# An RWKV-5 recurrence with a routed MoE behind it: in-place state decay, a gate on one partition, a split first block, the first-layer weights in one tile, a split last store and a new instruction order

## The chip, the cores and the metric

The kernel runs on one core of one Trainium2 chip. The metric is the device time of one execution in microseconds (us); less is better. A run more than 1.5% above the fastest of the same kernel is called slow, and only fast runs are compared with fast runs. A ratio quoted here is the mean time of the fast runs of one kernel over the mean time of the fast runs of the kernel before in the same rounds on the same chip, so it is not quite the ratio of the medians beside it.

Engine names in profile lines: PE is the matrix engine, PEld its weight loads, DVE the vector engine, ACT the scalar engine, POOL the GpSimd engine, SP the engine that queues most transfers (SPq is its queue).

## The reference, cut to what matters

```python
# r, k, v: [4, 8, 768, 48]; w, u: [8, 48]
for t in range(S):
    cur = einsum('bhd,bhe->bhde', u[None] * k_t, v_t)
    y[:, :, t] = einsum('bhd,bhde->bhe', r_t, state + cur)
    state = w[None, :, :, None] * state + einsum('bhd,bhe->bhde', k_t, v_t)
x = y as [4, 768, 384]
# one expert of eight for each batch element, chosen by the mean of x
logits = x.mean(axis=1) @ w_gate
e = argmax(logits); gate_w = softmax(logits)[e]
out = gate_w * (relu(x @ w1[e]) @ w2[e])      # w1: [8, 384, 1024], w2: [8, 1024, 384]
```

The inner einsum over `d` is a recurrence over 768 steps. The expert of a batch element is known only when its whole sequence is done.

## The kernel before

The sequence is cut into 12 blocks of 256 steps, three for each of the four batch elements. For each block the kernel scales `k` and `r` by powers of the decay, transposes them on PE (`t`, tile `twp`), copies them out (`kr`), computes scores on PE (`at`), multiplies them by a mask on DVE (`gt`, 1.2 us, the largest DVE operation), and adds up `y` and the state `s` on PE. When a batch element is done, the gate picks its expert, POOL issues the load of that expert's weights, and the two matmul layers of the expert (`mm1`, tile `hp`; `mm2`, tile `op`) run among the blocks of the following elements.

Every instruction is a step with a name, and a string, the order table, says in which order the steps are emitted on all engines:

```python
ORDER = """\
DVE k 0 0; DVE r 0 0; ACT late; fill 1 b0; PE t 0 0 b0; DVE k 0 1; DVE r 0 1; J k 0; J r 0
POOL r 1; fill 2 b1; PE t 0 1 b1; ACT kr 0 1; ACT v 0; DVE kr 0 0; fill 6 b2; PE at 0 0; DVE k 1
...                                   # some 90 more lines
```

Inside one engine the order is fixed; engines wait for each other by semaphores, which a framework places from the tiles and the address ranges that instructions touch. `fill` puts matmuls of zeros on PE to keep its clock up.

The parts that the change touches:

```python
def carried(g):                      # state of the last block back into PSUM
    nc.tensor.matmul(out=s_ps[b][:, 0 : 2 * D * NP], lhsT=ident,
                     rhs=carry[b]..., start=True, stop=False)

def state_out(g, o):                 # o = 1: the decayed state, as bf16
    st = work.tile([128, NP, 2 * D], BF16, tag="st")
    nc.vector.tensor_mul(st, s_ps[b]..., wcmask if o else bmask...)

def gate(b):                         # logits on all 128 partitions
    for ct in range(NCT):
        nc.tensor.matmul(out=lgp, lhsT=pools[b][:, ct : ct + 1].to_broadcast([128, 128]),
                         rhs=wg[:, ct, :], ...)

def weights(b):
    for fh in range(2):              # w1 in two tiles, each with its own transfer
        t = wpool.tile([128, NCT, HF], BF16, tag=f"w1_{fh}")
        nc.gpsimd.dma_start(out=t, in_=moe_w1[...][:, :, HF * fh : HF * fh + HF])
        w1s[b, fh] = t
    ...                              # w2 in one transfer

step(("fence",), {"SP": 0.5}, lambda e: nc.sync.dma_start(out=fence, in_=gws[0][0:1, :]), ...)
```

The fence is a tiny transfer that reads the gate weight of batch element 0. It stands in SP's queue ahead of the loads of blocks 7 to 9, so that these do not compete with the first expert's weights.

Of the kernel before, what the change touches and what calls it, by code (L numbers as in the profile page):

```python
# [19 lines left out]
DVE k 0 0; DVE r 0 0; ACT late; fill 1 b0; PE t 0 0 b0; DVE k 0 1; DVE r 0 1; J k 0; J r 0  # L20
POOL r 1; fill 2 b1; PE t 0 1 b1; ACT kr 0 1; ACT v 0; DVE kr 0 0; fill 6 b2; PE at 0 0; DVE k 1
DVE prod 0 0 b0; DVE prod 0 1 b1; DVE gt 0 0; PE t 1 0 b2; ACT kr 1 0; PE s 0 0; DVE st 0 1
PE bonus 0; PE t 1 1 b0; PE at 0 1; PE y 0 1 0; PE s 0 1; PE inter 0 1; ACT kr 1 1
DVE prod 1 0 b2; DVE gt 0 1; DVE prod 1 1 b0; POOL k 2; POOL r 2; DVE tcol 0; J vt 0; SP load 4
SP load 5; SP load 6; fill 2 b1; PE at 1 0; PE bonus 1; DVE tcol 1; DVE st 1 0; ACT v 1
POOL vt 1; DVE gt 1 0; PE t 2 1 b1; PE y 0 1 1; PE t 2 0 b2; PE carry 1; PE s 1 0; PE y 0 0 0
PE vt_y 0; PE at 1 1; DVE st 1 1; POOL k 3; POOL r 3; ACT kr 2 1; ACT kr 2 0; ACT xn 0 1
DVE gt 1 1; DVE prod 2 0 b2; DVE prod 2 1 b1; PE y 0 0 1; PE y 1 1 0; PE s 1 1; ACT xn 0 0
PE y 1 0 0; PE inter 1 0; PE at 2 0; DVE gt 2 0; PE y 1 0 1; PE inter 1 1; PE bonus 2
PE t 3 1 b0; PE at 2 1; PE turn 0 b2; DVE tcol 2; DVE st 2 0; POOL v 2; POOL vt 2; POOL k 4  # L30
POOL r 4; DVE gt 2 1; PE t 3 0 b1; PE vt_y 1; PE pool 0; PE carry 2; PE y 1 1 1; PE s 2 0
ACT v 3; ACT kr 3 1; ACT xn 1 0; ACT xn 1 1; DVE kr 3 0; DVE prod 3 1 b0; DVE st 2 1
DVE prod 3 0 b1; PE y 2 0 1; PE y 2 1 0; PE at 3 0; PE turn 1 b0; PE bonus 3; PE inter 2 1
PE y 2 0 0; PE y 2 1 1; PE vt_y 2; DVE gt 3 0; PE at 3 1; ACT v 4; ACT xt 0 b2; ACT xn 2 1
DVE tcol 3; DVE xt 1 b0; DVE gt 3 1; PE inter 2 0; ACT xn 2 0; PE t 4 1 b1; PE pool 1; PE pool 2
DVE gate_sums 0; PE t 4 0 b2; PE gate 0; ACT kr 4 1; ACT kr 4 0; DVE k 5; DVE choose 0
POOL vt 3; POOL r 5; POOL weights 0; ACT exp 0; fill 3 b0; PE at 4 0; DVE prod 4 0 b2
DVE prod 4 1 b1; DVE gt 4 0; POOL v 5; PE turn 2 b0; PE t 5 0 b2; ACT xt 2 b0; ACT kr 5 0
PE s 3 0; PE t 5 1 b1; ACT kr 5 1; DVE st 3 1; PE at 4 1; PE bonus 4; PE s 3 1; PE vt_y 3
PE inter 3 1; DVE gt 4 1; DVE st 4 0; DVE tcol 4; PE at 5 0; ACT xn 3 0; ACT xn 3 1  # L40
DVE prod 5 0 b2; DVE prod 5 1 b1; PE inter 4 0; PE carry 4; PE s 4 0; PE bonus 5
PE mm1 0 2 0 b0; PE mm1 0 3 0 b2; ACT relu 0 2 0 b0; PE mm1 0 2 1 b1; ACT relu 0 3 0 b2
ACT relu 0 2 1 b1; POOL k 6; POOL vt 4; DVE gt 5 0; DVE r 6; DVE tcol 5; PE mm1 0 0 0 b0
PE t 6 1 b2; PE t 6 0 b1; DVE st 4 1; DVE gw 0; DVE kr 6 1; DVE prod 6 1 b2; PE s 4 1; PE vt_y 4
PE at 5 1; DVE st 5 0; ACT relu 0 0 0 b0; ACT kr 6 0; DVE prod 6 0 b1; PE turn 3 b0
PE mm1 0 3 1 b2; ACT xt 3 b0; DVE xn 4 0; PE carry 5; PE mm1 0 6 0 b1; PE inter 4 1
PE mm1 0 4 0 b0; ACT relu 0 3 1 b2; DVE relu 0 6 0 b1; ACT relu 0 4 0 b0; PE inter 5 0
PE mm1 0 1 1 b2; ACT relu 0 1 1 b2; DVE gt 5 1; DVE xn 4 1; PE mm1 0 0 1 b1; PE mm1 0 5 1 b0
PE mm1 0 1 0 b2; ACT relu 0 0 1 b1; ACT relu 0 5 1 b0; PE s 5 0; DVE st 5 1; PE at 6 0
PE mm1 0 6 1 b1; DVE relu 0 1 0 b2; DVE gt 6 0; SP fence; SP load 7; SP load 8; SP load 9  # L50
PE mm1 0 7 1 b0; PE mm1 0 5 0 b2; DVE relu 0 7 1 b0; DVE r 7; ACT relu 0 6 1 b1
ACT relu 0 5 0 b2; POOL vt 5; POOL k 7; POOL r 8; PE mm1 0 4 1 b1; PE inter 5 1; PE s 5 1
PE at 6 1; PE vt_y 5; ACT v 6; ACT relu 0 4 1 b1; POOL k 9; DVE xn 5 1; PE mm1 0 7 0 b2
PE t 7 0 b0; PE pool 4; PE bonus 6; PE pool 3; PE mm2 0 5 0 b1; ACT relu 0 7 0 b2; DVE xn 5 0
DVE gt 6 1; PE pool 5; DVE gate_sums 1; PE mm2 0 5 1; DVE k 8; ACT v 7; ACT kr 7 0; PE gate 1
DVE choose 1; DVE prod 7 0 b0; PE mm2 0 1 0 b2; PE mm2 0 1 1; DVE tcol 6; ACT gated 0 5 b1
DVE vt 6; ACT gated 0 1 b2; PE t 7 1 b1; PE mm2 0 4 0 b0; PE mm2 0 4 1; PE t 8 0 b2; DVE kr 7 1
DVE prod 7 1 b1; ACT exp 1; ACT gated 0 4 b0; ACT kr 8 0; DVE r 9; PE s 6 0; PE at 7 0
PE turn 5 b1; ACT xt 5 b1; PE mm2 0 0 0 b0; PE mm2 0 0 1; DVE gt 7 0; DVE prod 8 0 b2
POOL weights 1; DVE gated 0 0 b0; PE bonus 7; PE t 9 1 b1; PE t 9 0 b2; PE t 8 1 b0; ACT v 8  # L60
ACT kr 8 1; DVE st 6 1; PE s 6 1; PE at 7 1; PE vt_y 6; ACT kr 9 0; ACT xn 6 0; DVE kr 9 1
DVE prod 9 1 b1; DVE tcol 7; DVE prod 8 1 b0; DVE st 7 0; DVE prod 9 0 b2; DVE gt 7 1; POOL vt 7
PE mm2 0 3 0 b1; PE mm2 0 2 0 b0; PE mm2 0 2 1; PE carry 7; PE inter 7 0; PE inter 6 1
# [52 lines left out]
def kernel(  # L116
# [250 lines left out]
    def transpose_by_dma(g, i):  # L367

        if g not in krs:
            kr_tile(g)  # L370
# [555 lines left out]
```

## Time and profile before

Three runs took 137.63 to 137.73 us. The first profile fell on an execution with a wait, which the prediction below takes out by calculation. A later profile of the same kernel (run e0 below, 137.75 us) serves as "before" from here on.

| part of the 137.75 us | us | how it is read |
|---|---|---|
| front: start of the span to the first expert matmul | 37.22 | start of the first `hp` row in PE's timeline |
| dense part: first expert matmul to the end of the last | 93.60 | 124.96 + 5.86 - 37.22 in the lines below |
| tail: last eviction and last store | 5.3 | the span, 136.1, less 130.82 |
| outside the span | 1.65 | 137.75 - 136.1 |

In PE's timeline the columns are start, duration, engine, line, operation, tiles, engine shape, sizes, count, and in brackets the idle time before it with what ended it.

```profile
37.22 2.14 PE L669 MATMUL hp<-xt,w 128*128 128x384 bf16 x12 [0.68 <-DMA w<-in_moe_w_dram]
```

The end of its chain of waits (start, duration, what):

```profile
124.96 5.86 PE op L688 x36
130.90 0.58 ACT ob L699
```

Twelve expert matmuls start together after a short wait of 0.68 us and run at full clock. The chain ends with one eviction by ACT, and the store follows.

### The profile page before, as it was taken

To read this page: it belongs to the slowest core of one execution; us is meant where nothing else is said; L and a number is where in the kernel's file an instruction comes from. 1 tells how busy PE (TensorE), PEld (TensorE's weight loads), DVE (VectorE), ACT (ScalarE), POOL (GpSimd) and SP (SyncE) were. 2 spreads that over 40 slices of the span, in tenths; PEclk is the share of its full clock that TensorE was granted. 3 is DMA by queue.
4 is the path that set the end of the run, shared out by engine and by line. 5 is a ranking of instruction groups with operands and counts; after the bars stand their busy time and mean duration, and the time that the engine had idled before them with its cause. 6 is when DMAs were issued, how large, how long until landed. Compare 5 with 4: busy or idle time off the path is not lost.

```text
span 139.8 us, 4473 instructions
## 1 busy us (share of the span) xinstructions
PE 129.2 (92%) x1928; PEld 89.4 (64%) x1928; DVE 98.5 (70%) x193; ACT 67.6 (48%) x119; POOL 55.2 (39%) x52
## 2 busy tenths in 40 slices
PE   6998999998589999999999999999999999999940
PEld 2256677876347676778767786686767756666620
DVE  6499999996946689988659978857756336683110
ACT  0986584677235747376446483073544600422130
POOL 4158599969940537142101963804120060000000
PEclk9999999999968999999999999999999999999997
DMA  2999997979999999089649992995006559980254
GB/s 47 293 325 325 285 237 198 244 205 247 206 209 240 237 293 280 1 105 212 137 95 270 319 271 72 128 212 115 5 0 170 172 80 191 235 284 5 66 130 144
DMA packets 46473, 25.47 MB, mean 182 GB/s; under 512 B 39284, under 2 KB 45429, under 8 KB 46453
## 3 DMA queue, kind: packets, MB, share of 16 engines
q1 hardware_dynamic: 41332, 18.89, 49.9%
q0 software_dynamic: 4288, 6.29, 26.3%
q8 instruction: 15, 0.25, 0.7%
q10 hardware_dynamic: 832, 0.00, 0.3%
q14 instruction: 6, 0.04, 0.2%
HBM read 26.76 MB, written 4.72 MB: 225 GB/s over the span
## 4 chain that ended last, share of the span: by engine, by line
PE 65%; SPq 15%; DMA 10%; DVE 3%; issue 2%; POOL 1%; ACT 0%; POOLq 0%; ACTq 0%
PE op L688 23%; PE hp L669 22%; SPq L176 14%; DMA w<-in_moe_w_dram 5%; DMA r<-in_r_dram 5%; PE twp L351 4%; PE y L498 3%; PE xp L582 2%; PE at L402 2%; PE s L526 2%; PE y L468 2%; PE y L486 1%; DVE rp L333 1%; PE s L616 1%; SPq L206 1%
## 5 line engine op out<-in xcount | busy, mean ns | idle before, releaser
L669 PE MATMUL hp<-xt,w 128*128 128x384 bf16 x192 | 37.8, 338 | 2.0 <-DMA w<-in_moe_w_dram 2.0
L680 ACT ACTIVATE ht<-hp 128x384 bf16<-128x384 f32 x45 | 21.5, 490 | 34.0 <-PE hp L669 34.0
L688 PE MATMUL op<-w,ht 128*128 128x384 bf16 x192 | 34.0, 326 | 0.0
L415 DVE TENSOR_TENSOR gt<-at,mask 128x1024 bf16<-128x1024 f32 x24 | 29.2, 1217 | 1.3 <-PE at L402 1.0
L669 PEld LDWEIGHTS <-w 128*128 128x128 bf16 x192 | 20.2, 115 | 10.9 <-DMA w<-in_moe_w_dram 2.0
L688 PEld LDWEIGHTS <-ht 128*128 128x128 bf16 x192 | 18.1, 98 | 11.0 <-DVE tcol L441 0.2
L333 POOL TENSOR_TENSOR kp<-k,dk 128x768 bf16<-128x768 f32 x8 | 14.7, 1841 | 15.6 <-DMA k<-in_k_dram 15.6
L446 POOL TENSOR_TENSOR vt<-vb,tcol 128x768 bf16<-128x768 bf16 x9 | 14.0, 1551 | 16.3 <-DVE tcol L441 11.5
L339 ACT COPY kr<-twp 128x1024 bf16<-128x1024 bf16 x16 | 16.0, 1014 | 6.9 <-PE twp L351 6.9
L333 POOL TENSOR_TENSOR rp<-r,dr 128x768 bf16<-128x768 f32 x7 | 12.7, 1818 | 5.9 <-DMA r<-in_r_dram 5.8
L701 DVE TENSOR_SCALAR ob<-op,gw 128x384 f32<-128x384 f32 x13 | 7.9, 615 | 9.5 <-PE op L688 9.4
L498 PE MATMUL y<-vb,gt 64*128 64x48 bf16 x384 | 14.4, 180 | 0.2
L498 PEld LDWEIGHTS <-gt 64*128 64x128 bf16 x384 | 11.4, 93 | 3.9 <-issue 2.6
L682 DVE TENSOR_SCALAR ht<-hp 128x384 bf16<-128x384 f32 x19 | 10.2, 554 | 5.4 <-PE hp L669 5.3
L699 ACT ACTIVATE ob<-op,gw 128x384 f32<-128x384 f32 x11 | 6.4, 581 | 14.3 <-PE op L688 14.3
L654 POOL DMA_DIRECT2D w<-in_moe_w_dram x8 | 6.4, 803 | 15.7 <-DVE xt L341 9.4
L351 PE MATMUL twp<-ident,rp 128*128 128x128 bf16 x96 | 9.5, 223 | 0.8 <-POOL rp L333 0.7
L390 DVE TENSOR_TENSOR prod<-twp,kr 128x512 bf16<-128x512 bf16 x24 | 9.7, 418 | 0.7 <-ACT kr L339 0.5
L351 PE MATMUL twp<-ident,kp 128*128 128x128 bf16 x96 | 9.6, 225 | 0.6 <-DVE kp L333 0.4
L526 PE MATMUL s<-vb,kp 64*128 64x96 bf16 x160 | 10.2, 204 | 0.0
L402 PE MATMUL at<-kr 48*64 48x128 bf16 x384 | 9.9, 220 | 0.3 <-DVE gt L415 0.2
L339 ACT CAST xn<-y 128x384 bf16<-128x384 f32 x15 | 6.9, 482 | 5.1 <-PE y L486 3.5
(75 smaller groups left out, 168.6 us busy)
## 6 DMA issues: line engine op xcount, KB each, us to landing
k<-in_k_dram SPq DMA_DIRECT2D x12, 384.0 KB, 5.1
r<-in_r_dram SPq DMA_DIRECT2D x12, 384.0 KB, 6.3
v<-in_v_dram SPq DMA_DIRECT2D x12, 384.0 KB, 5.6
out_dram<-ob SPq DMA_DIRECT2D x22, 192.0 KB, 3.4
w<-in_moe_w_dram POOLq DMA_DIRECT2D x8, 384.0 KB, 6.3
w<-in_moe_w_dram POOLq DMA_DIRECT2D x4, 768.0 KB, 10.1
out_dram<-ob SPq DMA_DIRECT2D x4, 96.0 KB, 2.1
wuT<-in_w_dram ACTq DMA_DIRECT2D x2, 0.8 KB, 2.8
```

The costliest lines, as they stand in the source:

```text
L176: nc.sync.dma_start(out=t.rearrange("q h c d -> q h (c d)"), in_=src[b, :, L * gi : L * gi + L, :].rearrange("h (q c) d -> q h (c d)", c=2),)
L333: eng.tensor_mul(dst[:, cs, :, 0:D].rearrange("q c h d -> q h c d"), src[:, :, cs, :], dec[:, :, cs, :])
L339: nc.scalar.copy(dst, src)
L351: nc.tensor.transpose(out=twp[:, o + p, :], in_=src[:, c, 2 * p : 2 * p + 2, :].rearrange("s a b -> s (a b)"), identity=ident,)
L402: nc.tensor.matmul(out=at[64 * j : 64 * j + 64, a, pp, cs, :].rearrange("q (c i) -> q c i", c=2), lhsT=kt[q, p, j, cs, :], rhs=rt[q, p, j] ...
L415: nc.vector.tensor_mul(gts[g][:, rnd].rearrange("q a p c t -> q (a p) (c t)"), ats.pop((g, rnd)).rearrange("q a p c t -> q (a p) (c t)"), ...
L446: eng.tensor_mul(vts[g], vbs[g].rearrange("q c h d -> q (c h) d"), src.to_broadcast([128, 2 * H, D]))
L498: nc.tensor.matmul(out=yj[:, D * h : D * h + D], lhsT=gt[q, p // 2, a, p % 2, c, :], rhs=vb[q, c, h, :], start=begin(g, j), stop=(c == 1), ...
L526: nc.tensor.matmul(out=sp[:, 96 * p : 96 * p + 96], lhsT=kp[g % NR][qo, c, 2 * p : 2 * p + 2, :].rearrange("s a b -> s (a b)"), rhs=vb[qo, ...
L669: nc.tensor.matmul(out=hp[:, 0:SB].rearrange("q (n l) -> q n l", l=C), lhsT=w1s[b, ft // 4][:, ct, ft % 4 :: 4], rhs=xts[b][:, 3 * sb : 3 ...
L680: nc.scalar.activation(out=o, in_=src, func=ACT.Relu)
L688: nc.tensor.matmul(out=moe_ps[b, si][:, 0:DM], lhsT=hts[b][:, ft, 128 * si : 128 * si + 128], rhs=w2s[b][:, ft, :], start=(ft == 0), stop= ...
```

## The change

The intent: save PE's identity matmuls that carry the state, and most of the gate's fp32 matmuls; start block 0 earlier; shorten the last store; and anneal the order table anew for the new durations. The table differs in nearly every line, so it is not shown. The core of the rest:

```diff
-def carried(g): ...                                  # identity matmul, 8 of them
+def decay(g):                                        # the state decays where it lies
+    sp = s_ps[g // NB][:, 0 : 2 * D * NP]
+    nc.vector.tensor_mul(sp, sp, wcmask...)
 def state_out(g, o, eng):
-    nc.vector.tensor_mul(st, s_ps[b]..., wcmask if o else bmask)
+    if o: copy(eng, st, sp)                          # bf16 copy, ACT or DVE
+    else: nc.vector.tensor_mul(st, sp, bmask...)

-    lgp = s_ps[b][:, ...];   lhsT=pools[b][:, ct : ct + 1].to_broadcast([128, 128])
+    lgp = s_ps[b][0:1, ...]; lhsT=pools[b][:, ct : ct + 1]
+def gate_spread(b, bank):                            # gate weight to 128 partitions
+    nc.tensor.matmul(out=gwp[b][:, 0:1], lhsT=one, rhs=gw1[b], start=True, stop=True)
+def gate_spread_out(b): nc.vector.tensor_copy(gws[b], gwp.pop(b)[:, 0:1])

-    for fh in range(2):
-        t = wpool.tile([128, NCT, HF], BF16, tag=f"w1_{fh}")
-        nc.gpsimd.dma_start(out=t, in_=moe_w1[...][:, :, HF * fh : HF * fh + HF])
-        w1s[b, fh] = t
+    t = wpool.tile([128, NCT, F], BF16, tag="w1")
+    for f in ([slice(0, HF), slice(HF, F)] if b == 0 else [slice(0, F)]):
+        nc.gpsimd.dma_start(out=t[:, :, f], in_=src[:, :, f])
+    for fh in range(2):
+        w1s[b, fh] = t[:, :, HF * fh : HF * fh + HF]

-    fence reads gws[0][0:1, :]
+    fence reads gw1[0]
... # block 0: scalings, transposes, copies and products by halves of the heads
... # last output: ACT and DVE evict 192 columns each, each half stored from another queue
... # x kept as [128, 3, 768] instead of by chunks; an output store is one transfer, not two
```

## The prediction

> **What bounds the kernel now.** I read the page first, then the timelines of TensorE (PE), VectorE (DVE) and GpSimd (POOL), then the chain of waits. From the page, busy shares and four rows of the forty slices (3.5 us each):
>
> ```profile
> PE 129.2 (92%) x1928; PEld 89.4 (64%) x1928; DVE 98.5 (70%) x193; ACT 67.6 (48%) x119; POOL 55.2 (39%) x52
> ...
> PE   6998999998589999999999999999999999999940
> ...
> DVE  6499999996946689988659978857756336683110
> ...
> PEclk9999999999968999999999999999999999999997
> DMA  2999997979999999089649992995006559980254
> ```
>
> The reader is to see two stages. From slice 3 to 10 DVE stands at 9 and so, nearly, does the DMA; there PE is busy partly with filler matmuls. From slice 13 on PE is at 9 throughout and DVE falls off. Between lies one hole, with a low clock after it. The timelines of POOL and PE show the hole:
>
> ```profile
> 30.15 1.82 POOL L333 TENSOR_TENSOR rp<-r,dr 128x768 bf16<-128x768 f32 x1 [1.06 <-DMA r<-in_r_dram]
> 31.95 1.71 POOL L654 DMA_DIRECT2D w<-in_moe_w_dram  x2
> ```
> ```profile
> 36.56 0.36 PE L432 MATMUL s<-U,prod 128*128 128x8 bf16 x8
> 38.87 3.71 PE L669 MATMUL hp<-xt,w 128*128 128x384 bf16 x12 [1.95 <-DMA w<-in_moe_w_dram]
> ```
>
> POOL scales the r of block 5 when its load lands, and only then issues the first expert's weights; they land 6.9 us later. PE waits 1.95 us for them, and its first twelve matmuls take 3.71 us where twelve at the later rate of 0.163 us (1.95 us for x12 in the chain) take 1.95: 1.76 us lost to a half clock. After that the chain is PE matmuls almost without a break, to the last output:
>
> ```profile
> 45.53 0.16 PE s L508
> ...
> 47.00 1.95 PE hp L669 x12
> ...
> 83.85 0.62 PE s L616 x6
> ...
> 134.59 0.58 ACT ob L699
> ```
>
> The profiled execution took 141.46 us (its span 139.8, so 1.66 lie outside the span) and the timed ones 137.65. Taking out both losses gives 139.8 - 1.95 - 1.76 + 1.66 = 137.75. So I read the timed runs as having neither the hole nor the slow clock: the DMA is faster without the profiler, and the weights are there when PE gets to them at 36.9. The three timed runs agree within 0.1 us, which also speaks against a wait on DMA. The timed run then is: 36.9 us of front, 95.65 - 1.76 = 93.9 us of dense PE (38.87 to 134.52, less the slow clock), 5.3 us of tail, 1.66 us outside.
>
> **What the Trainium skill says.** "TensorE: Matmul & The Clock Gate", section "LDWEIGHTS (loading the stationary operand)": the load costs by the columns of the stationary operand, not by its rows. The gate loads 128 fp32 columns at 190 ns each in this trace against 98 to 115 ns for 128 bf16 columns; with one column it should nearly vanish. The same page, "Why this matters for your kernels", asks for no PE gaps over about 3 us to keep the clock; here 1.95 us sufficed (granted clock 0.56 from 38.8 to 42.4), so the measurement decides. "PSUM — Partial Sum Buffer", "The four PSUM rules": writes of VectorE leave the accumulate bits alone, so the matmul after an in-place decay adds onto the decayed state; the kernel before never does this, so its trace shows nothing of it. "Trainium Kernel Development and Optimization", "Key Constraints": queues of several engines share the same 16 DMA engines, and issuing from several only saves issue time. In the trace a store of 96 KB costs some 0.6 us to issue, and the last output issues two in a row.
>
> **The change part by part.**
>
> Decay in place. It removes 8 identity matmuls that carry the state back into PSUM, 0.16 us each in the chain: 1.3 us of PE, 5 of them (0.8) after the first expert matmul. On DVE it is neutral: 8 multiplications of 0.55 us become 8 decays of the same shape. It adds 8 copies to bf16, 0.48 us each as ACT's casts of that size; the new order puts 6 on ACT (2.9 us for an engine that is 48% busy) and 2, of blocks 5 and 8, on DVE (0.55 each). The state's path gets one hop longer, which matters only in the front.
>
> Gate on one partition. Its six matmuls cost about 0.61 us in the chain; 0.13 us is what six one-column bf16 matmuls cost there (the pooling sums), so I put 0.25 for fp32. Saved: 0.36 x 4, three of them (1.1) late. The broadcast of the weight adds one fp32 matmul, by estimate 0.2 us (0.6 late), and one DVE copy of 0.17 us per batch. DVE's small operations keep their 0.13 to 0.17 us: they are fixed cost.
>
> Block 0 by halves of the heads. Before, the scores need both transposes copied out, and DVE puts the scaling of k1 (2.57 us beside POOL; 1.0 us when alone) and two products ahead of the first mask multiplication, which starts at 12.21 us. After, k1 is on POOL and half the heads suffice. But each half now needs both position columns of the decay table, so the first scaling waits for the third table activation, at 7.03 instead of 6.01. Step by step: four scalings of 0.52 us pitch to 9.2, one half copy of 0.45 to 9.65, product to 10.1, first mask at about 10.2: 2.0 us earlier.
>
> Order of the front. DVE binds there: 12.1 busy of the 12.6 us from 7.4 to 20. From its first mask multiplication to that of block 4's second half (start 33.87, end 35.1) it takes 22.9 us. I added up its list in the new order: 10 mask multiplications at 1.22, 9 products at 0.41 or so, 7 state operations at 0.55, the vt of blocks 0 and 2 at 0.95, v1 at 0.55, small ones 1.6: 23.4 us, of which 22 pass at the pitch of before (operations overlap by some 6%). xt 1, k5 and one kr copy have left DVE. So that mask ends at about 32.5 with half a microsecond of stalls, and PE is ready for the first expert matmul near 33.7 instead of 36.9. It also has less behind it: one group of y and s matmuls, one bonus and one inter group now come after that point, 0.50 + 0.18 + 0.17 = 0.85 us moved.
>
> The weights then bind. POOL must do k5 as well as r5 before it issues them, and the fence that held back loads 7 to 9 opens earlier, because the gate weight it waits for moves ahead in DVE's order (before, SP waited 8.8 us for it, until 40.1). So nothing speeds the landing except the earlier choice of the expert (about 28 instead of 30.3 by the same sums) and POOL's shorter list ahead. In timed runs they land by 36.9 at the latest before; I put 34.9 after, between 33.5 and 37.
>
> Dense part: 93.9 - 0.8 (carries) - 1.1 (gates) + 0.6 (spreads) + 0.85 (moved) = 93.45.
>
> Tail: the last output is evicted by two engines at once, 192 columns each: about 0.35 instead of 0.58 us, and the second issue of 0.6 us goes to another queue: 5.3 - 0.23 - 0.6 = 4.4 us.
>
> Sum: 34.9 + 93.45 + 0.3 (stalls for the second half of the weights, needed only some 2.6 us after the first) + 4.4 + 1.66 = 134.7 us, 2.1% less than before.
>
> **The rivals.** First, a hole in front of the experts: PE is ready 3 us sooner but the weights come as late as before (36.9). For it: POOL's k5, the early fence, DMA at 9 in that stretch, and the hole in the profiled run. Against it: the narrow timed runs. The front's gain is then void, and the total is 136.7; with a half clock after the hole another 1.7, so 138.4 at worst. Second, the front is not DMA-bound at all without the profiler and the weights land by 33.7: then 133.5, and near 132.5 if the new order also removes stalls later on. For it: the rate falls from 325 GB/s early on to about 200 to 240 later at the same busy share, as if something else, perhaps the profiler, took the engines' time. Third, DVE or ACT becomes the bound later, through 2.9 us more on ACT and the longer state path; against it, DVE is busy at most 13 of 15 us in any stretch after 45 us, ACT 8.7, and matmuls of the experts fill every wait. I give that at most 1 us.
>
> **Range and chances.** The certain part is the tail (0.9) and the leaner dense part (0.45 after the moved work): 1.4 us, 1%. The rest depends on the landing of the weights. The mark for 2% is 134.9, right at my number. I put 132.9 to 136.7 as the range of 8 in 10; faster by over 2%: 0.52; within 2%: 0.45; slower: 0.03.
>
> **What would show it.** In the profile after: the first mask multiplication near 10.2; no identity matmul between state updates; a gate of 0.25 us; the first expert matmul ready near 33.7 to 36 and a wait of 2 to 3 us for weights still there, as the profiler's runs have slow DMA, with a low clock behind it; 93 to 94 us from the first to the last expert matmul at full clock; a tail of 4.4 us. I am wrong if the first mask comes later than 11.5, if the weights land after 37 in timed runs, or if PE waits on DVE or ACT by more than 1 us in the dense part.

## The result, and the profile after

The changed kernel took 146.34 us (median of four; fast runs 145.40, 146.28, 146.40) against 137.64 for the kernel before in the same rounds. The ratio is 1.0615 with a 95% interval of 1.056 to 1.0671: slower by 6%. The prediction of 134.7 was wrong, and so was its range.

The page of the changed kernel, a fast run of 146.28 us (its span 144.6; one digit is the busy share in tenths of a slice of 3.6 us):

```profile
PE 130.1 (90%) x1927; PEld 89.3 (62%) x1929; DVE 93.2 (64%) x189; ACT 74.2 (51%) x136; POOL 58.4 (40%) x52
...
PE   6989989799319999999899999999999999999970
...
DVE  6275999989800587789966998894667614165120
...
PEclk9999999999955999999999999999999999999997
DMA  3999999995999894007999397089810069980043
```

PE has a hole in the eleventh and twelfth slice ("31"), and its clock is halved in the twelfth and thirteenth ("55"). DVE starves just behind it ("00"), for nothing comes from PE, while the transfers ("99894") are busy all along: something is being loaded, and PE waits for it. PE's timeline there:

```profile
37.89 0.35 PE L680 MATMUL hp<-xt,w 128*128 128x384 bf16 x1 [0.55 <-DMA w<-in_moe_w_dram]
42.79 2.75 PE L680 MATMUL hp<-xt,w 128*128 128x384 bf16 x8 [4.55 <-DMA w<-in_moe_w_dram]
```

Where the kernel before ran twelve expert matmuls in a row, here one runs, then PE waits 4.55 us for weights, and the next eight take 0.34 us each instead of 0.18. Counted from the second matmul the run divides so: front 42.79, dense part 97.3 (to 140.06), tail 4.5, outside the span 1.7; sum 146.3. Against the table of before that is +5.6, +3.7, -0.7 and 0.

The transfers in that stretch come from two queues. POOL's timeline of the changed kernel has the issue of the first expert's `w1`:

```profile
32.54 1.71 POOL L667 DMA_DIRECT2D w<-in_moe_w_dram  x2 [0.76 <-issue]
```

SP's queue in the changed kernel (start, duration of the issue, what):

```profile
32.91 0.69 SPq L923 DMA_DIRECT2D fence<-gw  x1
...
34.71 3.88 SPq L180 DMA_DIRECT2D v<-in_v_dram  x1
38.68 6.03 SPq L180 DMA_DIRECT2D k<-in_k_dram  x1
```

SP's queue in the kernel before, in its first profile:

```profile
40.10 0.70 SPq L888 DMA_DIRECT2D fence<-gw  x1
```

POOL issues the weights at 32.54, no sooner than before (31.89 in e0). The fence opens 7.2 us earlier than before, and from 33.65 on the loads of blocks 7 to 9 move together with the weights. The earlier front did not come either. PE's timeline before (e0) has the fillers and the first scores so:

```profile
9.83 1.46 PE L213 MATMUL fill<-zero 128*128 128x512 bf16 x6
11.22 0.42 PE L402 MATMUL at<-kr 48*64 48x128 bf16 x16
```

PE's timeline of the changed kernel, which puts the fillers between the two halves of block 0's scores:

```profile
10.64 0.64 PE L427 MATMUL at<-kr 48*64 48x128 bf16 x16
11.22 2.42 PE L218 MATMUL fill<-zero 128*128 128x512 bf16 x5
13.57 0.42 PE L427 MATMUL at<-kr 48*64 48x128 bf16 x16
```

A filler of the same size takes 0.24 us before and 0.48 us after: PE is still at half clock at 11 to 13 us, and the second half of block 0's scores waits behind these fillers.

So four things had to be explained: the wait of the second matmul, the early loads, the late front, and a dense part that is not shorter. My theory after reading: (1) the two halves of the first expert's `w1`, now in one tile and interleaved row by row, are taken for overlapping, so every matmul waits for both; (2) the early fence makes the weights land late; (3) the clock and DVE make the front late; (4) in the dense part other waits take the place of what was saved. The rivals: the weights are merely late whatever the tile; the transfers are slow for another reason; and in the dense part one single part of the change (decay, gate, or order of DVE) is to blame. The compiled instruction list spoke for (1): in the changed kernel the weight load of the second expert matmul, two instructions after the first, already waits for the second transfer.

```
after:   1195 Ldweights w1 [waits DMASW0]   1197 Ldweights w1 [waits DMASW1]
before:  1270 Ldweights w1_0 [waits DMASW0] 1434 Ldweights w1_1 [waits DMASW1]
```

### The profile page after: what moved, and what is told of

The parts are those of the page before. It is cut to its first block, busy times and chain, and to the rows that moved or that the text cites. A ratio compares the mean times of both kernels' runs of the same rounds, so it can differ in the third digit from the quotient of the medians.

```text
span 144.6 us, 4487 instructions
## 1 busy us (share of the span) xinstructions
PE 130.1 (90%) x1927; PEld 89.3 (62%) x1929; DVE 93.2 (64%) x189; ACT 74.2 (51%) x136; POOL 58.4 (40%) x52
## 4 chain that ended last, share of the span: by engine, by line
PE 59%; SPq 13%; DMA 12%; DVE 8%; POOL 2%; issue 2%; POOLq 0%; ACT 0%
PE hp L680 23%; PE op L698 19%; SPq L180 12%; DMA w<-in_moe_w_dram 6%; DMA r<-in_r_dram 4%; PE y L515 3%; PE twp L363 3%; DVE kp L338 2%; PE at L427 2%; DMA k<-in_k_dram 2%; PE xp L594 2%; PE y L493 2%; DVE gt L440 2%; PE s L535 1%; PE y L503 1%
## 5 line engine op out<-in xcount | busy, mean ns | idle before, releaser
L338 POOL TENSOR_TENSOR rp<-r,dr 128x768 bf16<-128x768 f32 x10 | 18.9, 1885 | 17.4 <-DMA r<-in_r_dram 17.4
L709 ACT ACTIVATE ob<-op,gw 128x384 f32<-128x384 f32 x17 | 9.9, 582 | 22.0 <-PE op L698 19.1
L472 POOL TENSOR_TENSOR vt<-vb,tcol 128x768 bf16<-128x768 bf16 x8 | 12.3, 1550 | 19.9 <-DVE tcol L467 19.8
L351 ACT COPY kr<-twp 128x1024 bf16<-128x1024 bf16 (+1 forms) x18 | 16.6, 945 | 5.7 <-PE twp L363 3.3
L692 DVE TENSOR_SCALAR ht<-hp 128x384 bf16<-128x384 f32 x22 | 12.1, 553 | 9.4 <-PE hp L680 9.4
L561 DVE TENSOR_TENSOR st<-s,bmask 128x384 bf16<-128x384 f32 x12 | 6.6, 548 | 9.3 <-ACT ht L690 7.8
L351 ACT CAST xn<-y 128x384 bf16<-128x384 f32 x20 | 9.2, 482 | 6.4 <-PE y L503 6.4
L218 PE MATMUL fill<-zero 128*128 128x512 bf16 x21 | 9.6, 555 | 1.7 <-DVE zero L189 1.3
L427 PEld LDWEIGHTS <-kr 48*64 48x64 bf16 x384 | 7.1, 108 | 3.4 <-issue 1.3
L535 PEld LDWEIGHTS <-kp 64*128 64x128 bf16 x160 | 8.0, 96 | 1.0 <-issue 0.8
```

Source lines behind the costliest of these rows:

```text
L338: eng.tensor_mul(dst[:, cs, :, 0:D].rearrange("q c h d -> q h c d"), src[:, :, cs, :], dec[:, :, cs, :])
L351: nc.scalar.copy(dst, src)
L427: nc.tensor.matmul(out=at[64 * j : 64 * j + 64, a, pp, cs, :].rearrange("q (c i) -> q c i", c=2), lhsT=kt[q, p, j, cs, :], rhs=rt[q, p, j] ...
L472: eng.tensor_mul(vts[g], vbs[g].rearrange("q c h d -> q (c h) d"), src.to_broadcast([128, 2 * H, D]))
L535: nc.tensor.matmul(out=sp[:, 96 * p : 96 * p + 96], lhsT=kp[g % NR][qo, c, 2 * p : 2 * p + 2, :].rearrange("s a b -> s (a b)"), rhs=vb[qo, ...
L692: nc.vector.tensor_scalar_max(o, src, 0.0)
```

## The experiments

Eighteen experiments ran, all with correct results. "Front" is the start of the first `hp` matmuls that run without a further wait for weights; "dense" is from there to the end of the last expert matmul; both are from the profiled run, which can be one of the slower runs of its kernel.

| run | what | median us | ratio to before | front | dense |
|---|---|---|---|---|---|
| e0 | kernel before | 137.75 (one run) | | 37.22 | 93.6 |
| after | the changed kernel | 146.34 | 1.0615 | 42.79 | 97.3 |
| e1 | after + halves of w1 laid apart | 145.26 (one fast run: 142.01) | | 39.06, then 2.17 wait | |
| e2 | after + late fence | 143.42 | 1.0359 | 40.66 | 96.9 |
| e3 | both | 140.89 | 1.0219 | 38.98 | 95.7 |
| f1 | e3 + five fillers fewer | 142.86 | 1.0368 | 40.33 | 95.4 |
| f2 | e3 + a mask ahead of a scaling | 142.03 (139.09 to 145.12; one fast run) | 1.0308 over all runs, slow ones too | 37.17 | 95.7 |
| h1 | e3 + one filler more | 139.29 | 1.0127 | 39.09, after 1.71 wait | 95.3 |
| i1 | h1 + that scaling on POOL | 141.00 | 1.016 | 39.27 (slow run) | 95.8 |
| j1 | h1 + gate on 128 partitions again | 140.91 | 1.0177 | 39.20 | 96.0 |
| j2 | j1 + state copies on DVE | 140.09 | 1.0127 | 39.33 | 95.9 |
| g1 | before + w1 in one tile | 142.03 | 1.0326 | 38.59 | 96.0 |
| g2 | before + decay in place, copies on ACT | 145.79 | 1.0584 | 41.56 | 96.5 |
| g5 | before + decay in place, copies on DVE | 140.38 | 1.0161 | 38.75 | 93.7 |
| g3 | before + gate on one partition | 142.97 | 1.033 | 36.74 | 97.8 |
| i3 | g3 + two spreads later | 139.69 | 1.0124 | 37.53 | 95.7 |
| h2 | before + split last eviction | 137.74 | 0.9989 | 37.55 | 93.6 |
| i2 | before + last store from two queues | 137.85 | 1.0018 | 36.71 | 94.0 |
| b2 | i3 + two queues | 139.16 | 1.0099 | 36.98 | 96.0 |

### The weights: e0, e1, e2, e3, g1

**e0**, no edit: the kernel before.

> The kernel before, unchanged, for a second profile, hopefully of a fast execution. My reading of its first profile was that timed runs have no wait for the first expert's weights and no half clock after it: the first expert matmul should start at 36.9 us or a little before, with a total near 137.6. If instead the profile again shows a wait of about 2 us and a first expert matmul at about 38.9 at a total near 137.6, my baseline for the front was wrong and the dense part is shorter than the 93.9 us I took.

Measured: 137.75 us, no hole, no slow clock, a wait of 0.68 us for the weights. The reading of the kernel before by calculation (36.9, 93.9, 5.3) was right to 0.3 us in each part. Its reason was not: the prediction thought transfers faster without the profiler, but e0 is a profiled execution too, and its wait is short all the same.

**e1**, the halves of the first `w1` contiguous in the same tile:

```diff
+        if b == 0:
+            t = t.rearrange("p c f -> p (c f)").rearrange("p (h c f) -> p h c f", h=2, c=NCT)
+            for fh in range(2):
+                nc.gpsimd.dma_start(out=t[:, fh], in_=src[:, :, HF * fh : HF * fh + HF])
+                w1s[b, fh] = t[:, fh]
```

> Only the first expert's w1 is laid out so that its two halves lie one after the other in the tile; in the changed kernel they interleave by rows, and the second expert matmul waits for the second half's transfer. Theory A (this false wait is most of the loss): the first three expert matmul groups run at 37.9 us, the second half is needed only at the fifth group near 40.5, where about 2 us of wait may remain since it lands at 42.8; total 146.3 - 2.6 - 1 = about 142.5. Rival B (the dense part after the start, with the decays and the longer state path, is to blame): the early start is given back and the total stays above 145. Rival C (the slow landing itself is to blame, not who waits for it): total 144 to 145.

Measured: three slow runs (144.85 to 146.3) and one fast one of 142.01. The profile is of a slow run, so only its order of events is used; PE's timeline:

```profile
39.06 1.65 PE L685 MATMUL hp<-xt,w 128*128 128x384 bf16 x9 [0.47 <-DMA w<-in_moe_w_dram]
44.15 1.17 PE L685 MATMUL hp<-xt,w 128*128 128x384 bf16 x6 [2.17 <-DMA w<-in_moe_w_dram]
```

Nine matmuls now run on the first half, and the wait for the second comes later; the compiled list puts that wait at instruction 1293 instead of 1197. The false wait is gone, and a true one of 2.17 us stands in its place, because the second half is late.

**e2**, the fence late, the tile as in the changed kernel:

```diff
-SP fence; SP load 7; SP load 8; SP load 9
-DVE xn 3 0; ACT xn 3 1; ...
+DVE xn 3 0
+SP fence; SP load 7; SP load 8; SP load 9; ACT xn 3 1; ...
-nc.sync.dma_start(out=fence, in_=gw1[0])
+nc.sync.dma_start(out=fence, in_=xns[3][0:1, 0, 0:2])
```

> The false wait stays, but the fence that holds back the loads of blocks 7 to 9 waits for block 3's y copy (37.4 us) instead of the gate's weight (32.7 us). Theory A with contention: the second half of w1 lands in about 7.3 us instead of 9.3, near 40.8, so PE waits 2 us less: about 144. If the loads do not slow the weights: no change, 146.3.

Measured: 143.42 us, ratio 1.0359. PE's timeline:

```profile
38.73 0.35 PE L680 MATMUL hp<-xt,w 128*128 128x384 bf16 x1 [1.90 <-DMA w<-in_moe_w_dram]
40.66 2.75 PE L680 MATMUL hp<-xt,w 128*128 128x384 bf16 x8 [1.57 <-DMA w<-in_moe_w_dram]
```

With the competing loads held back the second half is there 2.1 us sooner (40.66 against 42.79; POOL also issued the weights 0.5 us earlier in this run, so about 1.6 of it is left for the loads), but one matmul still runs alone and the clock is still halved behind it.

**e3**, both edits:

> Both edits. Theory A: no wait over 0.5 us for weights and no half clock after it: 146.3 - 4.6 - 2 = 139.5 to 140. Rival B: stays above 143. If it goes below 137.6 the rest of the change is a gain and the false wait is more than the whole loss.

Measured: 140.89 us, ratio 1.0219, interval 1.0166 to 1.0271. PE's timeline:

```profile
38.98 1.65 PE L685 MATMUL hp<-xt,w 128*128 128x384 bf16 x9 [0.29 <-DMA w<-in_moe_w_dram]
```

No hole and no halved clock are left. The two causes together cost 146.3 - 140.9 = 5.4 of the 8.7 us by which the changed kernel was slower.

**g1**, the one tile alone put into the kernel before (each batch element still in two transfers):

```diff
-            t = wpool.tile([128, NCT, HF], BF16, tag=f"w1_{fh}", name=f"w1_{b}_{fh}")
+        t = wpool.tile([128, NCT, F], BF16, tag="w1", name=f"w1_{b}")
+        for f in (slice(0, HF), slice(HF, F)):
+            nc.gpsimd.dma_start(out=t[:, :, f], in_=src[:, :, f])
```

> The kernel before, with only w1 put into one tile of 1024 columns, loaded in two halves for every batch: the false wait alone, in a kernel that is otherwise sound. The second expert matmul then waits for the second half, issued 0.85 us after the first and landing perhaps 1 to 1.5 us after it: 138.8 to 139.3, and near 140.5 if the half clock follows. If the false wait is not a cost by itself: 137.7.

Measured: 142.03 us against 137.70, ratio 1.0326. PE's timeline:

```profile
36.61 0.35 PE L668 MATMUL hp<-xt,w 128*128 128x384 bf16 x1 [0.44 <-DMA w<-in_moe_w_dram]
38.59 3.33 PE L668 MATMUL hp<-xt,w 128*128 128x384 bf16 x11 [1.62 <-DMA w<-in_moe_w_dram]
```

One matmul alone, a wait, then half clock: the signature of the changed kernel, in the kernel before, by this edit alone. The matmuls from the second on start at 38.59 instead of 37.22 (1.4 us), and eleven take 3.33 us, at the 0.18 us of e0 they would take 2.0 (1.4 us). With these 2.8 us the profiled run of 141.52 is explained up to 1 us, which I did not trace.

### The front: f1, h1

**f1** takes five of the six slow fillers away:

```diff
-... DVE gt 0 0; fill 6 b2; PE at 0 1
+... DVE gt 0 0; fill 1 b2; PE at 0 1
```

> On the repaired kernel (halves laid out apart, late fence; 140.9 us), five of the six filler matmuls that stand in PE's queue before block 0's second score group are taken out. They ran at about 0.48 us each and DVE waited 1.1 to 1.7 us for the scores behind them. Theory A (the fillers eat the start that the halves of the heads won): second mask multiplication about 1.5 us earlier than 15.0, first expert matmul about 1 us earlier, total near 139.9. Rival B: what follows waits for something else (v0, POOL's scalings, a colder clock), and the total stays within 0.5 us of 140.9.

Measured: 142.86 us, ratio 1.0368: slower than e3 by 2 us. The half clock stayed: scores at 18.94 us still took 0.64 us, where e3's took 0.40 from 18.5 on. The fillers were not only in the way, they brought the clock up. The idea of removing them was wrong.

**h1** does the opposite, one more filler at the start:

```diff
-... DVE r 0 0; fill 1 b0; PE t 0 0 b0; ACT kr 0 0 0
+... DVE r 0 0; fill 2 b0; PE t 0 0 b0; ACT kr 0 0 0
```

> On the repaired kernel (140.9 us), one filler matmul more before block 0's first transposes, where PE sits idle for 0.44 us. Theory A (the new order leaves PE just idle enough in the first 9 us that the full clock comes one window later, at 12.5 to 14.6 us instead of 9 to 10, so that the fillers and the scores behind them run at half rate): the six fillers run at 0.24 us each instead of 0.46, the second mask multiplication comes at about 13 instead of 15, and the total falls by 1 to 2 us, to about 139.3. Rival B (the clock's window is not moved by so little): fillers still at 0.46 us, total within 0.5 us of 140.9.

Measured: 139.29 us, ratio 1.0127 (1.0078 to 1.0176), 1.6 us better than e3. PE's timeline:

```profile
11.42 1.47 PE L218 MATMUL fill<-zero 128*128 128x512 bf16 x6
12.91 0.42 PE L427 MATMUL at<-kr 48*64 48x128 bf16 x16
```

The six fillers take 0.24 us each, as before the change, and the second half of the scores comes at 12.91 instead of 14.53 in e3. The size of this gain is not fixed: across the profiled runs that start comes at 13.11 to 14.53 without the extra filler (the changed kernel, e1, e2, e3, f2) and at 12.38 to 12.91 with it (h1, i1, j1, j2), so the direction is clear and the 1.6 us is one pair. The clock seems to go in whole steps of time: its halved stretches last 3.41 us in e2 and g1 and 6.83 us, twice that, in the changed kernel. That a little more work early on can win a whole step is inferred from these lengths, not tested.

The experts of h1 start no earlier than e3's for another reason:

```profile
39.09 1.65 PE L685 MATMUL hp<-xt,w 128*128 128x384 bf16 x9 [1.71 <-DMA w<-in_moe_w_dram]
```

PE was ready at 37.38 (in e3 at 38.69) and then waited 1.71 us for the weights, so the weights bound there, as in the prediction's first rival. The profiled run, 140.72 us, is the slowest of h1's four; the others took 139.05 to 139.53. That they lack this wait is likely, but they have no trace. No halved clock followed this wait.

Yet even with the clock right, PE was ready no earlier than before (37.38 against 36.54 in e0). The DVE timeline of h1 shows why:

```profile
8.52 2.17 DVE L345 TENSOR_TENSOR rp<-r,dr 128x384 bf16<-128x384 f32 x1
...
15.93 1.26 DVE L353 CAST vb<-v 128x768 bf16<-128x768 f32 x1
...
23.93 2.61 DVE L472 TENSOR_TENSOR vt<-vb,tcol 128x768 bf16<-128x768 bf16 x1
...
35.06 1.22 DVE L440 TENSOR_TENSOR gt<-at,mask 128x1024 bf16<-128x1024 f32 x1
```

POOL's timeline of the same run has the other half of the story:

```profile
8.44 1.83 POOL L338 TENSOR_TENSOR kp<-k,dk 128x768 bf16<-128x768 f32 x1 [1.99 <-DMA k<-in_k_dram]
...
23.92 1.80 POOL L338 TENSOR_TENSOR kp<-k,dk 128x768 bf16<-128x768 f32 x1
```

The scaling of r took 0.55 us in the changed kernel's own profile, where it began 0.44 us ahead of POOL's operation; here POOL began 0.08 us ahead of it (8.44 against 8.52), and it takes 2.17 us; the `vt` multiplication takes 2.61 us instead of 0.95; the cast 1.26 instead of 0.55. The Trainium skill says so in "SBUF — State Buffer", section "SBUF: two separate sides": DVE and POOL share one pair of ports under an exclusive lock, which a DVE operation needs when it reads two inputs from SBUF against a POOL operation that also reads there, or when it runs in a mode that uses both port pairs; whichever starts first holds it for its whole instruction. The trace agrees: the `vt` that starts 0.01 us after POOL's scaling ends 0.82 us after that scaling does, at 26.54, about the 0.95 us that it takes alone. The three together cost 1.6 + 0.7 + 1.7 = 4.0 us in DVE's list.

### The decay: g2, g5

**g2** puts the in-place decay into the kernel before and lets ACT make the copies, right behind each decay:

```diff
-DVE tcol 1; DVE st 1 0; ACT v 1 ... PE carry 1; PE s 1 0
+DVE tcol 1; DVE dec 0; ACT st 1 0; ACT v 1 ... PE s 1 0
```

> The kernel before, with only the decay in place: 8 identity matmuls of 0.16 us less on PE, 8 copies of 0.48 us more on ACT, each right behind its decay; the rest of the order as it was. Theory A (my prediction's part): 0.8 us less in the dense part, little change in the front: near 136.9. Rival B (the longer path of the state, decay then copy then the next state matmuls, stops PE): 138 or more.

Measured: 145.79 us, ratio 1.0584. ACT's waits in this run (who waited for whom: us in total, times, longest):

```profile
ACT st L339 <- DVE s L547: 10.3, 5, 3.8
```

A copy at the head of ACT's queue waits up to 3.8 us for its decay, and every eviction behind it waits too. PE then loses its clock for 6.83 and 3.41 us, and the front grows to 41.56. This is a placement that I chose, not the changed kernel's, so it says only that the copies are dangerous on ACT.

**g5**, the same with the copies on DVE:

```diff
-DVE dec 0; ACT st 1 0
+DVE dec 0; DVE st 1 0
```

> The kernel before with the decay in place as in the run that came out at 145.8, but the copy of the state on DVE right behind its decay instead of on ACT. Theory A (in that run the copy stood at the head of ACT's in-order queue while its decay was not done, and held up what stood behind it): total falls to 138.0 to 138.8, the rest being 8 more operations of 0.55 us on DVE, three of them in the front, against 1.3 us less on PE. Rival B (the in-place decay itself, a longer path from state to state, costs the time): stays above 143.

Measured: 140.38 us, ratio 1.0161. The front is 1.5 us longer (38.75), for DVE binds there and has three more copies. The dense part is 93.7, as before (93.6), although the five identity matmuls are gone. Summing PE's times from each start to the next start, the carries give back 1.10 us, and the groups `hp`, `twp` and `op` grow by 0.82, 0.30 and 0.09. Of the growth of `hp`, 0.63 is one wait of an expert matmul at 43.6 us for a product of DVE; no wait of the state update shows. In this order, on its own, the decay in place gains nothing, because another wait for DVE takes what it saves.

### The gate: g3, i3, j1, j2

**g3** puts the gate on one partition, with its spread, into the kernel before:

```diff
-DVE gw 0; ...
+DVE gw 0; ... PE gwb 0 b2; DVE gws 0 b2       # likewise for the other three
-lhsT=pools[b][:, ct : ct + 1].to_broadcast([128, 128])
+lhsT=pools[b][:, ct : ct + 1]
```

> The kernel before with only the gate on one partition, and the broadcast of its weight by one fp32 matmul and a copy. The dense part of the repaired kernel shows the gates 1.1 us cheaper than before and the broadcasts costing 0.9 us (counted from start to next start on PE), so the net should be 0.3 to 0.5 us less here: 137.3. My prediction had 0.5 us less in the dense part and 0.16 in the front. If the fence, which now opens with the weight of one partition, or the waits around the broadcast matter: 138 or more.

Measured: 142.97 us, ratio 1.033. The dense part is 97.8 us, 4.2 longer. The gate's six matmuls became cheap as predicted: from start to next start 1.13 us less for the three in the dense part. (The load of a one-column fp32 operand took 81 ns against 190 for 128 columns: less, but it does not nearly vanish, as the prediction had it.) But the spread is one more wait of PE for DVE. The biggest single wait of PE in this run:

```profile
PE op L698 <- DVE ob L711: 1.9, 1, 1.9
```

An expert's output matmul waits for a PSUM bank that DVE has not emptied; by my reading because the spread took a bank and a turn in DVE's queue. **i3** moves the spreads of batch elements 1 and 2 some steps later:

```diff
-PE mm1 1 1 0 b0; PE gwb 1 b2; DVE gws 1 b2; PE s 7 1
+PE mm1 1 1 0 b0; PE s 7 1 ... PE mm1 1 3 1 b1; PE gwb 1 b2; DVE gws 1 b2; DVE gt 8 1
-PE mm2 1 5 1; PE gwb 2 b2; DVE gws 2 b2; DVE kr 10 0
+PE mm2 1 5 1; DVE kr 10 0 ... DVE v 11; PE gwb 2 b2; DVE gws 2 b2
```

> As the gate run that came out at 143.0, but the broadcasts of batches 1 and 2 stand later in PE's order, where the weight is long there. Theory A (that run's loss was PE standing at a broadcast whose weight was not there, and the order behind it): back to 137.3 to 137.8. Rival B (the gate on one partition costs by itself): stays above 140.

Measured: 139.69 us, ratio 1.0124; the dense part is 95.7. Half of the dense part's loss (97.8 to 95.7) was the place of the spread, and 3.3 of the 5.2 us by which the median rose. The other half of the dense part's loss, 2.1 us over before, stays in this order. The costliest groups of PE in the expert stretch (36 to 136 us; busy us, mean ns of one) have the gate of the kernel before, e0, as:

```profile
L616 PE MATMUL s<-wg,pooled 128*128 128x8 f32 x18 | 2.2, 245 | 0.0
```

The same view of i3 has the spread and the gate:

```profile
L648 PE MATMUL gwp<-gw,one 1*128 1x1 f32 x8 | 1.5, 252 | 0.3 <-DVE ht L692 0.2
L616 PE MATMUL s<-wg,pooled 128*1 128x8 f32 x18 | 0.9, 170 | 0.0
```

The gate falls from 2.2 to 0.9 us busy, and the spread, recorded as two instructions for each weight (eight in this window, which holds all four), brings back 1.5.

So I suspected the gate in the changed kernel too. **j1** undoes it there, from h1:

```diff
-PE gwb 0 b2; ... DVE gws 0 b2; ...            # and the other three
-lgp = s_ps[b][0:1, TC + 6 * H : TC + 6 * H + E]
+lgp = s_ps[b][:, TC + 6 * H : TC + 6 * H + E]
-lhsT=pools[b][:, ct : ct + 1]
+lhsT=pools[b][:, ct : ct + 1].to_broadcast([128, 128])
```

> The kernel of h1_warm (the changed kernel with the halves of the first weights laid apart, the late fence and one more filler: 139.29 us, 1.0127) with one part of the change undone: the gate's logits are computed on 128 partitions again, and the matmul that spreads the weight, with its copy, is gone; nothing else is moved. Theory A, the gate on one partition is what makes the dense part long: in the kernel before it alone took the dense part from 93.7 to 95.8 us even when spread later, so here the dense part from the first to the last expert matmul falls from 95.5 to 93.4-94.2 and the total to 137.2-138.2 (ratio 0.996-1.004). Theory B, several parts each cost a little, or the dense part is one of anticipating waits whatever is in it: dense 95.0-95.8, total 138.6-139.6 (1.007-1.014). Third: the six matmuls of the gate themselves come back at 0.61 us each group, so if the spread cost nothing net, the total rises to 140-140.6 (1.018).

Measured: 140.91 us, ratio 1.0177 (1.0095 to 1.0259), the dense part 96.0, 0.7 longer than in h1. Theory A falls: in the order of the changed kernel, undoing the gate does not shorten the dense part. By starts on PE, it takes away the spreads (0.93) and 0.47 of `op`, brings back 1.07 of the gate, and waits elsewhere grow (`twp` by 0.63, `hp` by 0.22). What the part costs depends on the order that it is put into. **j2** moves four state copies of j1 from ACT to DVE:

```diff
-DVE dec 6; ACT st 7 0         # likewise st 4, st 10, st 11
+DVE dec 6; DVE st 7 0
```

> j1_gate_back with the bf16 copies of the decayed state of blocks 4, 7, 10 and 11 on VectorE instead of ScalarE. If copies waiting at the head of ScalarE's queue hold back the evictions behind them (theory A; it was seen at 3.8 to 10.3 us each when the decay alone was put into the kernel before), the dense part is 0.5 to 1 us shorter than in j1 and the total 0.5 to 1 us lower. If the copies on ScalarE cost nothing in this order (theory B, they waited only 1.8 us in sum in h1_warm), the time stays within 0.4 us of j1, or is up to 0.6 us longer because VectorE has 2.2 us more to do.

Measured: 140.09 us, ratio 1.0127 (1.007 to 1.0185), the dense part 95.9. The profiled runs of j1 and j2 took 141.44 and 141.41; the medians differ by 0.8 with overlapping intervals. The copies on ACT are not what makes the dense part long either. In both profiled runs the clock was halved for 3.41 us in the front, in h1's it was not, so the totals of j1 and j2 do not compare simply with h1's; the dense parts do.

### DVE beside POOL in the dense part: f2, i1

In the changed kernel one scaling, `k 9`, meets POOL's work in the middle of the dense part; DVE's timeline, where the same operation for r alone took 0.94:

```profile
63.83 0.94 DVE L338 TENSOR_TENSOR rp<-r,dr 128x768 bf16<-128x768 f32 x1
...
67.11 3.27 DVE L338 TENSOR_TENSOR kp<-k,dk 128x768 bf16<-128x768 f32 x1
```

**f2** puts the mask multiplication behind it ahead of it, **i1** gives the scaling to POOL:

```diff
-DVE k 9; DVE gt 7 1          # e3
+DVE gt 7 1; DVE k 9          # f2
```
```diff
-POOL v 9; DVE k 9; DVE gt 7 1             # h1
+POOL k 9; POOL v 9; DVE gt 7 1            # i1
```

> On the repaired kernel, the mask multiplication of block 7's second half goes ahead of the scaling of k9 in DVE's order; that scaling takes 3.2 us there because POOL works beside it. Theory A (the stall of the dense part, from about 58 to 66 us in the chain, is this one): PE's wait of 0.6 us and the chain through DVE vanish, total 1 us or more lower, about 139.9. Rival B: the dense part is longer for many small reasons and this one gives under 0.4 us.

> On the repaired and warmed kernel (139.3 us), the scaling of k9 goes from DVE, where it took 3.2 us beside POOL in a stretch in which DVE is busy 14 of 15 us, to POOL, which later waits 11 us for a load. Theory A (what the dense part lost, 95.5 us instead of the 93.45 predicted, comes from DVE being the bound in that stretch): dense part 94 to 94.5, total about 138.2. Rival B (PE's in-order queue meets other waits of the same size, as when only the mask was moved ahead): dense part stays at 95.4 or more, total at 139.3.

Measured: f2 spread from 139.09 to 145.12 us (median 142.03); the ratio of 1.0308 (interval 1.0239 to 1.0378) is over all four runs, of which three are slow, and the one fast run, 139.09, is about 1.009 of before. In its profile, the run of 139.09, the dense part is 95.7, the same as in e3, and the wait that vanished at the scores appears elsewhere (0.7 us of `hp` for a product). i1 took 141.00 us, its fast runs 138.83 and 140.72, ratio 1.016 (1.0084 to 1.0236), and its profiled run, a slow one, has a dense part of 95.8. Neither move made the dense part shorter. The 3.27 us operation looked guilty, but taking its wait away only moved the wait elsewhere.

### The tail: h2, i2, b2

**h2** evicts the last output by halves on two engines, in the kernel before, and stores it from two queues; **i2** does only the two queues; **b2** is i3 with two queues.

```diff
-DVE gated 3 0 b1; ACT gated 3 1 b0; SP store 3 0                                 # before
+DVE gated 3 0 b1; SP store 3 0 0; DVE gated 3 1 1; ACT gated 3 1 0; J gated 3 1 b0; SP store 3 0 1   # h2
```
```diff
-for c in range(2):         nc.sync.dma_start(out=dst[c]..., in_=obs[b, gi][64 * c : ...])
+for c, eng in ((0, nc.sync), (1, nc.scalar)): eng.dma_start(...)                  # h2, i2, b2
```

> The kernel before with only the tail changed in the same spirit: the last output is evicted by ACT and DVE, half the columns each, and its two transfers go out from two queues at once; the first of the last two outputs is stored as soon as it is there. Predicted saving 0.8 us and a little for the smaller last store: 136.8. If the landing of the last transfer sets the end whatever its issue: 137.6.

> The kernel before, its last store of two transfers issued from SP and ACT side by side, evictions unchanged. In the changed kernel the two half evictions run one after the other (ACT waits for DVE), so what its tail won should be the issue alone. Theory A: tail 0.6 us shorter, 137.1. Rival B: the transfers share the engines and land no earlier, 137.7.

> The kernel before with the later broadcasts and the two queues for the last store: the attempt at a version better than both. If both parts hold: 136.7 to 137. If the gate is worth nothing: 137.1 to 137.3. If it is no better than 137.7 the change has no part that helps this kernel without a new order.

Measured: h2 137.74 us, ratio 0.9989 (0.9956 to 1.0022); i2 137.85, ratio 1.0018; b2 139.16, ratio 1.0099. None gains. The end of h2's chain:

```profile
131.21 0.43 DVE ob L710
131.71 0.42 ACT ob L708
```

The two halves of the eviction run one after the other. The changed kernel does the same:

```profile
140.09 0.43 DVE ob L723
140.54 0.42 ACT ob L721
```

The compiled list has ACT's half waiting for a semaphore of DVE. The Trainium skill would have told me: "PSUM — Partial Sum Buffer", section "PSUM bank collisions raise a hardware error", has ACT and DVE kept apart in one bank even when both only read and touch disjoint columns. The list of this kernel fits that, though it does not say whether the wait stands there for the bank; and the two halves of 0.43 + 0.42 us take longer than the one eviction of 0.58. i2 agrees with what the prediction cites on queues, that a second queue saves issue time only: the last issue ended 1.4 us after the last matmul instead of 2.0 in e0, and the tail stayed at 5.3. The changed kernel's tail is nevertheless 0.7 us shorter (4.5 against 5.3). What remains of the change there is that a store is one transfer over 128 partitions instead of two over 64; I did not test that alone.

## Why the prediction was wrong, point by point

**What bounds the kernel now: right.** Front, dense part and tail of the kernel before were 37.2, 93.6 and 5.3 in e0, against 36.9, 93.9 and 5.3 by calculation.

**The weights, 34.9 us and 0.3 us of stalls: wrong, and this is the step that failed first.** The prediction took the second half as "needed only some 2.6 us after the first". The first matmul started at 37.89, not 34.9: the choice of the expert came at 30.97, not about 28 (30.38 in the kernel before), POOL issued the weights at 32.54, and PE itself was ready only at 37.3. The second matmul then waited 4.55 us, not 0.3, and a half clock followed. In the changed code both halves lie in one tile with their rows interleaved, and the second matmul waits for both. g1 shows this edit alone makes the kernel before 3.3% slower. The code was there to read, and the compiled list, which was to be had before the prediction, showed the wait at instruction 1197. The first rival named a hole with a half clock and put it at "138.4 at worst"; its mechanism was right, and its size was not, because it knew of one late landing and not of two that add up.

**The early fence: seen, and not counted.** The prediction names it and says only that nothing speeds the landing. e2 and e3 show what it costs: 146.34 to 143.42 with the false wait in place, and with the halves apart (one fast run of 142.01, so roughly) to 140.89. The two repairs overlap, since either shortens the same hole; together they give 5.4 us.

**First mask at 10.2 and PE ready near 33.7: wrong.** In the changed kernel the first mask came at 11.34 and PE was ready at 37.3 (37.89 less its wait of 0.55). Two terms were missing. The clock: the new order has less PE work at the start and reached full clock later; h1 gained 1.6 us by one filler. The list of DVE: the prediction's items add up to 23.8 us, not to its 23.4, which is small beside the miss. It counted 0.95 for each `vt` and 0.55 for the cast, the times alone, although it had itself noted a scaling of 2.57 us beside POOL against 1.0 alone. In h1, with the clock right, the last front mask ended at 35.06 + 1.22 = 36.3, 3.8 later than the predicted 32.5. The three DVE operations beside POOL exceed their counted times by 4.0, which is all of it. e3 shows the same three at 2.17, 1.64 and 1.98 us. In the changed kernel's own profile the last front mask ends at the same time, 36.29, but from other parts: the scaling of r took 0.55 there, DVE waited 1.01 and 1.14 us for scores at half clock, and the cast and `vt` exceed their count by 1.72. So the 4.0 us hold for h1 alone. This is read from profiles, not tested by an experiment that moves the three.

**Dense part, 93.45: wrong by about 2.** The savings were there: in h1 the carries are worth 1.10 and the gate 1.13 by starts on PE, where 0.8 and 1.1 were predicted. The spreads cost 0.93 (predicted 0.6). The work moved behind the first expert matmul, with the very counts of the prediction (16 `y`, 8 `s`, 8 bonus and 4 inter matmuls), came to 1.37, not 0.85. These four terms, predicted at -0.45, sum to +0.07. The rest of the 1.75 us by which h1's dense part (95.3) exceeds e0's (93.6) lies in other groups: `y` from `vt` 0.70 for the same 32 matmuls, `op` 0.50, `hp` 0.25, 0.2 in others. Times from start to start include waits: 0.6 of the growth of `y` is one wait for the mask that f2 and i1 moved, and the 0.50 of `op` is gone in j1 (0.03), so it came with the spreads. The prediction gave such waits "at most 1 us" in its third rival. I tried the gate (j1), the copies (j2), the one long scaling (f2, i1): none is the cause by itself, as the dense part stayed between 95.3 and 96.0 in every repaired version. By elimination the new order as a whole is left, which was only argued: the new order without the other parts was not run. What makes the repaired dense part long stays open to that extent.

**Tail, 4.4 us: right in size, wrong in reason.** It was 4.5 (the prediction's own sum, 5.3 - 0.23 - 0.6, gives 4.47). That the size fits is luck: the split eviction did not run on two engines at once, and two queues gave nothing in the kernel before.

**The sum.** The repaired kernel's best runs (h1, 139.05 to 139.53) stand 1.2 to 1.7 us above the median of the kernel before in the same rounds (137.82). Nothing that I ran beats the kernel before: h2 and i2 equal it.

## What to carry to other kernels

When tiles are merged, ask of each half not only where it lies but what range of addresses it spans: interleaved halves make each reader wait for both writers, and the compiled waits show it without a chip. Before counting a DVE operation at its time alone, look at what POOL does at that moment. And a saving on the busiest engine is only a saving when the thing that it now waits for comes earlier as well: here 2.2 us of matmuls went away and the dense part grew.

## What the Trainium skill lacked or had wrong

- "TensorE: Matmul & The Clock Gate", section "Why this matters for your kernels": it asks for no gaps over about 3 us. Here waits of 1.95 us (first profile of the kernel before) and of 1.62 us (g1) were each followed by a halved stretch of 3.41 us, and one of 1.71 us (h1) was not.
- The same page, Part 1, gives the warm-up as a small share of a kernel's time not worth fitting. Here one filler matmul of 0.43 us at the start moved the second half of the scores from 14.53 to 12.91 us and the total from 140.89 to 139.29, 1.1% (in other pairs of profiles the move differs: 13.11 to 14.53 without it, 12.38 to 12.91 with it).
- No page has that a matmul which reads one half of a tile can wait for a transfer into the other half, if the halves interleave: 4.55 us in the changed kernel, 1.62 us in g1.
- "SBUF — State Buffer" has the lock between DVE and POOL; it gives no durations for such pairs as these. Measured: scaling 2.17 us instead of 0.55, `vt` 2.61 instead of 0.95, cast 1.26 instead of 0.55, scaling of a whole block 3.27 instead of 0.94.
